# A new table of order for a fused attention and maxout-FFN kernel

## The chip, the core and the metric

The kernel runs on one core of one Trainium2 chip. The metric is the device time of one execution in microseconds (us); a kernel's time is the median of its runs. Lower is better.

## What is computed

Linear attention with learned features, then a feed-forward layer whose hidden value is the maximum of three products.

```
# q, k, v: (8, 8, 576, 64); w_phi: (64, 128)
proj = x @ w_phi                               # x is q or k
proj = proj - max(abs(proj), axis=-1)
phi  = concat(exp(proj), exp(-proj))           # 256 features
kv   = phi(k).T @ v;  z = sum(phi(k))
attn = phi(q) @ kv / (phi(q) @ z + 1e-6)       # per head
x    = attn as (4608, 512)
h    = maximum(maximum(x @ w1, x @ w2), x @ w3)   # 512 -> 768
out  = h @ w_out                               # 768 -> 512, float32
```

## The kernel before

**Units and stages.** Attention works in 16 units of four heads (half of a batch's eight), 18 tiles of 128 rows each. Of a unit, q, k and v are loaded; q and k are made bf16 and transposed into `qkT` (units 0 to 3 on PE at L494 and L497, with q and k of units 1 to 3 loaded straight into bf16 by POOL's queue at L463; later units by a cast on POOL at L480 and a transposing DMA at L512). PE projects (`G`, L535, into `psq` and `psk`), DVE takes the maxima (L554), ACT the exponentials of k (`Ek`, L548), POOL multiplies v by the rows' scale `em` (L589, into `vab`), PE forms `kvps` (`K`, L643: 72 matmuls of 65 columns), PE projects q once more (`M`, L614 to L619, into `psm`) with the maximum taken off, ACT takes the exponentials `Eq` (L627), PE multiplies by kv (`N`, L661, 10 matmuls into `psn`), DVE divides (L667, L668, into `x_sb`). The result is turned into `xT`, for units 0 and 1 on PE (`X`, L681) and a copy (L684), later by a transposing DMA (L691).

**The feed-forward part** runs over nine chunks of 512 tokens: one per batch (tokens 0 to 511 of 576) and one of all the rests. It uses max(a, b, c) = a + max(0, b - a, c - a). So w2 and w3 become differences with w1 (`wd`, L784, three instructions each, in place in `w_bf`), and w1 times w_out is formed once (`wt`, L798 and L801; `wm`, L812). A chunk has a first pass of six tiles with w2 - w1 (`up`, L714, evacuated with a relu at L722 or L724), a second with w3 - w1 (`up2`, L714, evacuated at L720), and per 128 tokens 4 matmuls with w1·w_out (L741) and 6 with w_out (L746) into one bank, a copy (L754) and a store (L761). Chunk 0 needs units 0 and 1 in `xT`, and the differences.

**What sets the order.** The program first makes a list of nodes (a node is a group of instructions on one engine, with its data and buffers). Then `plan` (L251) reads the table `PLAN`: each word is a node's number, a letter for its engine (T is PE, D DVE, A ACT, G POOL, S SP's queue), a digit for each buffer or PSUM bank that it is the first to use, and behind the @ a planned start. The words' sequence is the order in which the instructions are written, and so the order of each engine, which works in order; nothing is reordered on the chip. The planned starts are used for one thing more: where they leave PE a gap, `fill` writes matmuls on constant data (`idler`, L843), which keep PE running.

```
for word in PLAN.split():
    what, start = word.split("@")
    at = next(i for i, c in enumerate(what) if c.isalpha())
    n, slots = nodes[int(what[:at])], iter(what[at + 1:])
    n.eng, n.start = {"T": "PE", "D": "DVE", "A": "ACT", "G": "POOL", "S": "SP"}[what[at]], float(start)
    ...
    order.append(n)
```

**Loads.** SP's queue brings the raw q, k and v (L449, L474); POOL's queue brings q and k of units 1 to 3 (L463) and the four weight matrices (L421) with a cast to bf16. v of units 1 to 3 waits for a one-element copy on DVE (L472) that reads `qkT` of the unit before.

Of the kernel before, what the change touches and what calls it, by code (L numbers as in the profile page):

```python
# [105 lines left out]
1078G@20.80 106A@20.83 108D@20.83 70T070@20.95 96A@21.32 160D2@21.44 167D@21.54 161S@21.69 94D@21.76 109D@21.98 100T64@22.05
296S0@22.17 115T53@22.27 101A@22.52 72D@22.59 362S1@22.65 1094T2@22.75 119D@22.96 102A@23.02 117A@23.50 104D@23.66 116A@23.84
1096T0@24.05 107A@24.18 103D@24.26 124A1@24.68 118D@24.87 120A@24.93 127G1@25.07 71A@25.18 1095D@25.21 183T003400@25.44
1097A@25.59 173T16@25.66 168T57@25.88 123A@26.09 177D@26.13 1098T2@26.23 185A@26.24 170A@26.73 186D@26.74 125G@27.00 175A@27.22
176D@27.35 137T01@27.52 184A@27.71 171D@27.95 77T30@27.98 126G@28.12 138A@28.23 1092T1@28.29 78D0@28.56 139A@28.71 172D@29.18  # L110
1099A@29.20 122G@29.23 79T5@29.58 174A@29.70 187D@29.79 75T3@29.90 1093A@30.18 140T0@30.21 121G@30.35 229D3@30.39 131T2@30.44
76D1@30.50 141A@30.69 73T6@30.89 142A@31.03 80D0@31.11 128T4@31.21 132A@31.37 11G@31.47 364G0@31.62 74D1@31.73 178T13@31.76
133A@31.85 143T105@31.98 130A@32.34 181D@32.35 129A@32.82 182D@32.96 188T26@33.08 233T1@33.31 145A@33.33 192D@33.57 144A@33.73
134T4@33.88 191D@33.91 196A0@34.13 234D0@34.25 146T51@34.34 190A@34.38 198G0@34.53 148T0@34.65 135A@34.72 147D0@34.90
235T2@35.06 231T1@35.17 189A@35.20 149D1@35.52 199A@35.55 136A@35.70 152T5@35.74 193T6@36.05 232D@36.14 179A@36.18 81T0@36.29
83T4@36.60 197G@36.62 169A@36.67 153D0@36.76 150T1@36.91 194A0@37.16 154T7@37.31 236D@37.38 180A@37.41 195S@37.56 151D1@37.60
242T115611@37.72 84A@37.90 247T23@38.05 155D@38.22 297S0@38.34 156T1@38.39 82D@38.69 230S@38.82 215T047@38.87 157A@38.95
1080D@39.16 426S1@39.30 249A@39.60 1081D@39.78 1104T0@40.09 244A@40.09 1082D@40.40 248A@40.58 1106T1@40.95 250D@41.02 216A@41.07
365G@41.37 251D@41.63 1102T4@41.81 1107A1@42.06 246D@42.23 1105A@42.56 366S1@42.64 1110T2@42.67 245D@42.84 243A@43.06
1084D@43.45 1108T3@43.54 1103A@43.55 1111A@44.05 1085D@44.07 252T10@44.50 217A@44.55 1083D@44.69 257T56@44.72 237T42@44.83  # L120
1109A@44.95 1112T7@45.17 240D@45.31 259A@45.45 299G2@45.66 239A@45.79 255D@45.91 1124T3@46.04 254A@46.28 1113D@46.52 253A@46.77
1422G@46.78 1116T4@46.90 260D@47.13 300G@47.18 238A@47.26 1125D@47.47 556S0@47.65 258A@47.75 209T10@47.76 262T7@47.98
1118T5@48.04 241D@48.09 263A1@48.29 429G1@48.30 211A@48.54 264S@48.69 261D@48.70 212T3@48.90 203T7@49.01 210A@49.02 1117D@49.04
1120T2@49.23 363S0@49.47 204A@49.51 1119D@49.66 427S1@49.95 205A@49.99 200T6@50.09 256D@50.28 1122T1@50.30 214A@50.48
1121D@50.89 265A1@51.04 206T4@51.17 213A@51.29 266G1@51.44 367T005700@51.48 1123D@51.51 202A@51.63 301S2@51.63 382T02@51.70
1114T3@52.04 201A@52.11 386D@52.17 370D@52.78 1130T1@52.91 384A@52.93 1115D@53.39 208A@53.42 267G@53.53 224T60@53.77 207A@53.91
371D@54.01 220T5@54.08 383A@54.39 275T31@54.40 1131T@54.61 385D@54.62 369A@54.88 225D0@55.22 368A@55.37 1101G@55.62 221D1@55.84
276A@55.86 222T4@55.90 491S1@56.07 218T2@56.22 1132A0@56.35 223D0@56.47 272T0@56.53 278T6@56.74 268G@56.82 273A@56.99
372T75@57.06 219D1@57.09 430G@57.10 284T114@57.28 277A@57.48 376D@57.70 226S@57.85 274A@57.96 375D@58.31 377T23@58.38 280A@58.45
1126T0@58.72 286D@58.92 279A@58.93 380D@59.30 373A@59.42 281T7@59.58 387T46@59.79 285D@59.91 282A@59.94 269T2@60.06 1127T@60.27  # L130
283A@60.28 381D@60.29 431S0@60.52 271A@60.62 391D@60.89 270A@61.11 390D@61.23 293T11@61.56 395A0@61.59 374A@61.84 291T7@61.87
396G0@61.99 294D0@62.12 289T4@62.19 379A@62.33 1134T2@62.50 290D1@62.75 1128A1@62.82 287T5@63.36 292D0@63.37 388A@63.43
1138T1@63.68 378A@63.77 288D1@63.99 397G@64.08 389A@64.26 317T114011@64.64 295S@64.76 302T73@64.86 312T65@65.08 319A@65.11
320D@65.11 1135T@65.42 313A@65.60 321D@65.75 303A@66.09 559G0@66.18 316D@66.35 304A@66.58 1139T@66.71 557S0@66.88 305D@66.96
1136A2@67.07 398G@67.30 298S1@67.36 306D@67.57 1100G@67.58 314A@67.68 392T4@68.00 307T72@68.16 318A@68.17 315D@68.17
414T053@68.38 308A@68.66 1140D3@68.78 309A@69.15 393D0@69.40 322T06@69.48 310D@69.60 1142T1@69.71 394S@69.75 323A@69.84
324A@70.18 311D@70.21 416A@70.52 622S1@70.53 1154T4@70.57 560G@70.68 325D@70.82 1143A0@70.92 1129S@71.01 326D@71.16 415A@71.42
# [12 lines left out]
461G@91.60 353D1@91.66 572T47@91.79 1170T2@92.13 574A@92.26 359D0@92.28 579A@92.75 357D1@92.90 1171T@93.00 573A@93.24 575D@93.52  # L150
# [724 lines left out]
```

## Time and profile before

| | |
|---|---|
| median of 3 runs | 285.09 us (285.10, 285.09, 283.02) |
| span of the profiled execution | 282.5 us, first to last instruction; no other time of that execution is on the page |
| busy: PE, weight loads, DVE, ACT, POOL | 96%, 54%, 75%, 68%, 40% |
| granted TensorE clock | 1.000 |
| HBM | 34.64 MB read, 9.44 MB written, 156 GB/s over the span |

A row of a group or of the timeline names the line, the engine, the operation and out<-in; behind it stand the idle time of the engine ahead of it and what ended that. PEld is PE's loading of weights, which overlaps its matmuls. "issue" is time in which the engine waited for nothing that the profile shows. SPq, POOLq and ACTq are the issuing of DMAs.

### The profile page before, as it was taken

What the parts mean: (1) busy time and instruction counts of PE and PEld (TensorE: products, weight loads), DVE (VectorE), ACT (ScalarE), POOL (GpSimd) and SP (SyncE); (2) the same over time, 40 slices, a digit from 0 to 9 for tenths busy, and PEclk for the clock granted to TensorE, in tenths of its full rate; (3) what the DMA queues carried; (4) which work ended last, traced back from release to release, by engine and by line L of the source; (5) the groups of instructions that cost most, each with busy time, mean ns of one, the idle gap of its engine ahead of it and who ended that gap; (6) DMA issues with size and microseconds to landing.
All of it is one profiled execution on the core that took longest, in us unless ns stands there. A gap on an engine that the chain in (4) does not pass through costs nothing.

```text
span 282.5 us, 8556 instructions
## 1 busy us (share of the span) xinstructions
PE 271.2 (96%) x3521; PEld 154.0 (54%) x3560; DVE 211.6 (75%) x443; ACT 192.3 (68%) x449; POOL 113.2 (40%) x106
## 2 busy tenths in 40 slices
PE   8888979999999999999999999999999999999995
PEld 3565764566555644764556456555455465444443
DVE  4998989998877888679989876997477594254141
ACT  2897979898889779998585879977707961311111
POOL 8373567748176418913760563053033600000000
PEclk9999999999999999999999999999999999999999
DMA  7999999888999999999797866954975105600154
GB/s 202 240 206 282 280 273 240 266 204 167 300 363 198 175 308 300 194 165 277 212 199 129 246 235 124 166 102 167 186 177 116 40 4 104 137 2 0 37 123 139
DMA packets 68337, 51.45 MB, mean 182 GB/s; under 512 B 48778, under 2 KB 53066, under 8 KB 68298
## 3 DMA queue, kind: packets, MB, share of 16 engines
q1 hardware_dynamic: 63876, 45.74, 66.8%
q0 software_dynamic: 4000, 4.92, 10.0%
q8 instruction: 28, 0.46, 0.7%
q10 hardware_dynamic: 422, 0.24, 0.3%
q14 instruction: 11, 0.09, 0.1%
HBM read 34.64 MB, written 9.44 MB: 156 GB/s over the span
## 4 chain that ended last, share of the span: by engine, by line
PE 80%; DMA 11%; DVE 4%; issue 2%; SPq 1%; DVEq 0%
PE ups L714 31%; PE ops L746 14%; PE ops L741 10%; DMA wout_bf<-in_moe_w_out_dram 6%; PE psn L661 6%; PE kvps L643 5%; PE psm L614 5%; PE psq L535 4%; PE pm L812 2%; DMA out_dram<-osb 2%; DMA xT<-x_sb 2%; DVE x_sb L668 2%; DMA k_raw<-in_k_dram 1%; DVE mqp L554 1%; DVE mk L554 1%
## 5 line engine op out<-in xcount | busy, mean ns | idle before, releaser
L714 PE MATMUL ups<-xT,w_bf 128*128 128x512 bf16 x416 | 100.3, 379 | 1.4 <-DMA xT<-x_sb 0.3
L589 POOL TENSOR_TENSOR vab<-v_raw,em 128x1152 bf16<-128x1152 f32 (+1 forms) x36 | 68.2, 1907 | 67.2 <-ACT em L585 50.9
L548 ACT ACTIVATE Ek<-psk 128x512 bf16<-128x512 f32 (+1 forms) x160 | 80.8, 569 | 13.9 <-PE psk L535 10.1
L627 ACT ACTIVATE Eq<-psm 128x512 bf16<-128x512 f32 (+1 forms) x160 | 79.2, 570 | 7.3 <-PE psm L614 7.0
L714 PEld LDWEIGHTS <-w_bf 128*128 128x128 bf16 x432 | 41.0, 98 | 47.4 <-issue 0.4
L554 DVE TENSOR_REDUCE mqp<-psq 128x4 bf16<-128x512 f32 (+1 forms) x80 | 48.8, 631 | 6.3 <-PE psk L535 4.4
L746 PE MATMUL ops<-wout_bf,hT 128*128 128x512 bf16 (+2 forms) x215 | 49.3, 367 | 1.0 <-issue 0.5
L554 DVE TENSOR_REDUCE mk<-psk 128x4 f32<-128x512 f32 (+1 forms) x80 | 48.5, 628 | 2.4 <-PE psk L535 1.7
L720 DVE TENSOR_TENSOR hT<-hT,ups 128x512 bf16<-128x512 bf16 x54 | 36.1, 682 | 16.4 <-PE ups L714 12.7
L668 DVE TENSOR_TENSOR x_sb<-psn,rden 128x320 bf16<-128x320 f32 x64 | 31.5, 492 | 2.2
L746 PEld LDWEIGHTS <-hT 128*128 128x128 bf16 x228 | 21.1, 98 | 21.7
L722 ACT ACTIVATE hT<-ups 128x512 bf16<-128x512 f32 x33 | 19.1, 603 | 17.3 <-PE ups L714 15.8
L661 PEld LDWEIGHTS <-Eq 128*128 128x128 bf16 x640 | 25.0, 97 | 7.8 <-ACT Eq L627 0.2
L754 DVE COPY osb<-ops 128x512 f32<-128x512 f32 (+1 forms) x22 | 14.7, 669 | 16.8 <-PE ops L746 16.0
L661 PE MATMUL psn<-kv_sb,Eq 128*128 128x65 bf16 x640 | 26.9, 194 | 0.2 <-DVE mqp L554 0.2
L754 ACT COPY osb<-ops 128x512 f32<-128x512 f32 (+2 forms) x16 | 8.9, 562 | 23.2 <-PE ops L746 22.6
L741 PE MATMUL ops<-xT 128*128 128x512 bf16 x90 | 24.1, 380 | 0.3
L535 PE MATMUL psq<-w,qkT 64*128 64x128 bf16 x288 | 24.3, 217 | 0.1
L535 PE MATMUL psk<-w,qkT 64*128 64x128 bf16 x288 | 24.0, 217 | 0.4 <-ACT Eq L627 0.4
L535 PEld LDWEIGHTS <-qkT 64*128 64x128 bf16 x576 | 16.5, 94 | 12.0 <-issue 8.9
L614 PE MATMUL psm<-qkT,wphi_m 128*128 128x512 bf16 (+1 forms) x70 | 22.1, 358 | 0.0
L480 POOL CAST qk_bf<-q_raw 128x1152 bf16<-128x1152 f32 x12 | 13.8, 1147 | 20.3 <-DMA out_dram<-osb 9.4
(73 smaller groups left out, 230.9 us busy)
## 6 DMA issues: line engine op xcount, KB each, us to landing
v_raw<-in_v_dram SPq DMA_DIRECT2D x16, 576.0 KB
out_dram<-osb SPq DMA_DIRECT2D x64, 128.0 KB
q_raw<-in_q_dram SPq DMA_DIRECT2D x12, 576.0 KB
k_raw<-in_k_dram SPq DMA_DIRECT2D x12, 576.0 KB
w_bf<-in_moe_w_dram POOLq DMA_DIRECT2D x3, 768.0 KB, 20.3
qk_bf<-in_k_dram POOLq DMA_DIRECT2D x3, 288.0 KB, 13.9
qk_bf<-in_q_dram POOLq DMA_DIRECT2D x3, 288.0 KB, 13.4
wout_bf<-in_moe_w_out_dram POOLq DMA_DIRECT2D x1, 768.0 KB, 17.7
```

The lines of the kernel that those rows point to most:

```text
L535: nc.tensor.matmul(ps()[:, i, :], lhsT=cols[r, :], rhs=w2[r, c, :], start=True, stop=True)
L548: nc.scalar.activation(Ek[s]()[:, tiles_of(t0, n), :], of(1), EXP, scale=1.0 - 2.0 * s)
L554: nc.vector.tensor_reduce((mq, mk)[c]()[:, tiles_of(t0, n)], of(c), AXX, ALU.max, apply_absolute_value=True)
L589: (nc.vector if n_.eng == "DVE" else nc.gpsimd).tensor_tensor(vab()[:, g, t0:t1, 0:D], vb()[:, t0:t1, :], em()[:, g, t0:t1].unsqueeze(2).t ...
L614: nc.tensor.matmul(psm()[:, 0:w], lhsT=wphi_m, rhs=rhs, start=True, stop=True)
L627: nc.scalar.activation(Eqb()[s][:, cols], psm()[:, 0:w], EXP, scale=1.0 - 2.0 * s)
L661: nc.tensor.matmul(psn()[:, c, :], lhsT=Eqb()[g][:, t0:t0 + P], rhs=kv()[:, pr, ab, g, :], start=(g == 0), stop=(g == 1))
L668: nc.vector.tensor_tensor(x_sb()[:, pr, :, ab, :], psn()[:, :, 0:D], rden().to_broadcast([P, 5, D]), ALU.mult)
L714: nc.tensor.matmul(ups(), lhsT=w_bf[i + 1][:, ct, j * P:(j + 1) * P], rhs=tokens_of(ct), start=(ct == 0), stop=(ct == CT - 1))
L720: nc.vector.tensor_tensor(hT()[:, j, :], hT()[:, j, :], ups(), ALU.max)
L741: nc.tensor.matmul(ops_()[:, 0:width], lhsT=tile_of(ct, tt), rhs=line_w[c_i > MOVE][:, ct, cols], start=(ct == 0), stop=False)
L746: nc.tensor.matmul(ops_()[:, 0:width], lhsT=hT()[:, j, tt * P:(tt + 1) * P], rhs=wout_bf[:, j, cols], start=False, stop=(j == JT - 1))
```

## The change

Only the table is replaced. The new one was found by a search of small moves in plays of the program in which each transfer comes as late against plan as it did in a trace. Stages, tiles, buffers and every line of code are as before. A line of each, with the word for the load of w2 (node 1077):

```
-49G@14.45 41D@14.56 65A@14.63 43A@15.12 99D@15.16 110T67@15.27 63A@15.46 50G@15.57 55T5@15.61 98D@15.77 1077G@15.85 111A@15.94
...
+1093A@29.53 186D@29.89 77T6@29.97 138A@30.03 1077G@30.27 128T0@30.29 174A@30.52 78D1@30.54 178T47@30.86 129A@31.02 365G0@31.07
```

Of 1478 nodes 110 change engine: of the relus of the first pass 30 stand on DVE (21 before) and 24 on ACT (33), of the copies of L754 16 on DVE (22) and 22 on ACT (16), of the 14 copies to `mT` 10 on DVE (2), and the three `wd` of w3 on POOL (all six on DVE before).

On POOL, where w2 and w3 are loaded (the last two rows of L421), before:

```order
L589 TENSOR_TENSOR vab<-v_raw,em 128x9x64
L599 CAST vab<-em 128x2x9
L421 DMA w_bf<-in_moe_w_dram 128x4x768
L589 TENSOR_TENSOR vab<-v_raw,em 128x9x64 x2
L599 CAST vab<-em 128x2x9
L421 DMA w_bf<-in_moe_w_dram 128x4x768
L599 CAST vab<-em 128x2x9
L589 TENSOR_TENSOR vab<-v_raw,em 128x9x64 x4
```

The same place now, up to the differences of w3:

```order
L463 DMA qk_bf<-in_q_dram 128x2x576
L599 CAST vab<-em 128x2x9
L589 TENSOR_TENSOR vab<-v_raw,em 128x9x64 x4
L421 DMA w_bf<-in_moe_w_dram 128x4x768
L480 CAST qk_bf<-k_raw 128x18x64
L421 DMA w_bf<-in_moe_w_dram 128x4x768
L480 CAST qk_bf<-q_raw 128x18x64
L589 TENSOR_TENSOR vab<-v_raw,em 128x18x64 x2
L599 CAST vab<-em 128x36
L787 CAST gated<-w_bf 1x1 x3
L784 TENSOR_TENSOR w_bf<-w_bf 128x4x256 x3
```

Both loads moved behind unit 1's four multiplications, the second behind a cast too, and three subtractions came to POOL; one load of unit 3 (first row) also moved back, from ahead of unit 0's multiplications.

On DVE, from the last copies to `xT` to the reductions of unit 3, before:

```order
L684 COPY xT<-pxT 128x576 x2
L784 TENSOR_TENSOR w_bf<-w_bf 128x4x256 x3
L554 TENSOR_REDUCE mqp_80<-psq 128x4
L554 TENSOR_REDUCE mk<-psk 128x4 x2
L554 TENSOR_REDUCE mqp_80<-psq 128x4
L784 TENSOR_TENSOR w_bf<-w_bf 128x4x256 x3
```

And now:

```order
L554 TENSOR_REDUCE mqp_80<-psq 128x4
L784 TENSOR_TENSOR w_bf<-w_bf 128x4x256 x2
L554 TENSOR_REDUCE mk<-psk 128x4
L472 CAST v_raw<-qkT 1x1
L784 TENSOR_TENSOR w_bf<-w_bf 128x4x256
L554 TENSOR_REDUCE mk<-psk 128x4
```

The copies to `xT` went to ACT, the differences of w2 stand between reductions of unit 3, and those of w3 are gone from here.

On PE, rows 1213 to 1220 of its order (loads and matmuls counted from 0), in the turning of units 0 and 1; `Eq_1_77` and `Eq_1_78` are unit 1's exponentials of q. Before:

```order
L681 LDWEIGHTS x_sb
L681 MATMUL pxT<-ident,x_sb 128x128
L681 LDWEIGHTS x_sb
L681 MATMUL pxT<-ident,x_sb 128x128
L681 LDWEIGHTS x_sb
L681 MATMUL pxT<-ident,x_sb 128x128
L661 LDWEIGHTS Eq_1_77
L661 MATMUL psn<-kv_sb,Eq_1_77 128x65
```

Rows 1209 to 1216 now:

```order
L681 LDWEIGHTS x_sb
L681 MATMUL pxT<-ident,x_sb 128x128
L843 LDWEIGHTS idle
L843 MATMUL idler<-idle 128x512
L843 LDWEIGHTS idle
L843 MATMUL idler<-idle 128x512
L661 LDWEIGHTS Eq_1_77
L661 MATMUL psn<-kv_sb,Eq_1_77 128x65
```

Unit 0's ten transposes ran in one go before the last `N` of unit 1; now one group of five stands before another `N`, and two idlers between the second group and the last `N`.

More of the change, by code (lines that the diff above doesn't have):

```diff
@@ L106 @@
[L106 to L113, printed above, removed]
@@ new lines @@
+1160T1@79.91 328D1@80.01 403A@80.16 1159D@80.21 329S@80.36 407A@80.65 1156T0@80.78 1161D@81.03 686S1@81.06 404A@81.13
+622S1@81.52 406A@81.62 411T4@81.65 1162T7@81.77 1157D@81.90 494G@82.04 409A@82.10 333A@82.59 399T6@82.64 1163D@82.89
+349T115@82.96 401A@83.11 561S1@83.11 400A@83.62 452T20@84.00 412A@84.10 437T37@84.12 455D@84.37 350A@84.44 1174T6@84.45
+456D@84.71 413A@84.84 441D@85.05 351A@85.18 334T21@85.32 1175T@85.54 440D@85.66 439A@85.81 336A@86.30 335A@86.80 428S3@86.83
+346T1@86.84 419T40@86.96 1176D0@87.09 337T5@87.28 438A@87.29 343T3@87.50 420D0@87.71 1166T2@87.72 348A@87.78 1177S@87.86
@@ new lines @@
+1023A@205.52 1020D@205.76 1339T@205.83 1021D@206.36 1019A@207.12 1330T6@207.13 1340D1@207.38 1028A@207.61 1030D@208.00
+1327T@208.00 1341S@208.15 1025D@208.61 1031D@209.22 872T4@209.30 876T0@209.62 873D0@209.87 1331T@209.94 1029A@209.97
+877D1@210.49 1328D0@211.11 880S@211.26 1037T24@211.34 999T050@211.46 1038A@211.71 1040D@211.73 1018A@212.05 1032T12@212.50
+1332A3@212.54 1329S@212.76 1334T7@212.83 1035D@212.98 1024A@213.15 1041D@213.59 1335T@213.70 1036D@213.93 1039A@214.08
+1001A@214.42 1034A@214.82 1348T1@215.00 1336D2@215.25 990T61@215.87 1026D@215.87 1337S@216.02 1346T4@216.09 1045A1@216.62
@@ new lines @@
+1000A@216.87 996T0@216.96 1046G1@217.02 1350T7@217.08 1347D1@217.21 1333S@217.22 1349A@217.27 998A@217.77 984T3@217.95
+1042T5@218.17 1351D@218.20 1342T4@218.23 986A@218.42 1043D1@218.81 1344T1@219.10 1047G@219.12 1044A@219.16 1343D@219.35
+997A@219.86 1061T70@219.97 1052T5@220.09 1033A@220.20 1345D@220.22 1352T4@220.31 1053A@220.69 992A@221.17 993T1@221.18
+1428G@221.21 1354T0@221.40 1048G@221.61 1054A@221.66 991A@222.14 1064T125@222.36 1353A@222.63 995A@223.13 1362T6@223.49
+1065D@223.65 1066A@223.65 1355D@224.03 985A@224.05 1058T4@224.36 1062A@224.54 1055T2@224.58 1364T5@224.80 1057A@225.05
@@ new lines @@
+1389D@258.48 1434T3@259.10 1401D@259.11 1411T@259.97 1435D@260.22 1438T6@261.27 1412A0@261.52 1415T@262.14 1413S@262.28
+1439A@262.39 1444T1@263.44 1381S@263.48 1416A2@263.69 1440T4@264.31 1417S@264.68 1446T6@265.18 1441D@265.43 1419T@266.05
+1447D@266.30 1445D@266.92 1450T3@267.35 1420A3@267.60 1454T5@268.22 1421S@268.36 1451D@268.47 1453D@269.09 1458T4@269.09
+1459T@269.96 1455T@271.26 1460A0@271.51 1461A@272.14 1407T@272.56 1456D1@272.81 1457S@273.58 1462T6@273.86 1408D2@274.11
+1463T@274.73 1409S@274.88 1470T1@276.03 1471T@276.25 1464A3@276.28 1466T2@276.58 1472D0@276.83 1465A@276.91 1467T@277.01
@@ L245 @@
+1473A@277.51 1474T3@277.66 1475T@277.88 1468D1@277.91 1469S@278.45 1476A2@278.45 1477A@278.72
 """
```

265 lines of the change are left out of this document (126 added, 139 removed).

## The prediction

> **What bounds the kernel now.** I read the page first, then the busy time by stretch, then single rows.
>
> ```profile
> span 282.5 us, 8556 instructions
> PE 271.2 (96%) x3521; PEld 154.0 (54%) x3560; DVE 211.6 (75%) x443; ACT 192.3 (68%) x449; POOL 113.2 (40%) x106
> PE   8888979999999999999999999999999999999995
> PEclk9999999999999999999999999999999999999999
> 0.00:41.78 41.78, 36.75 (x715) 24.75 (x718) 34.53 (x84) 31.74 (x77) 24.00 (x33) 1.00 1.07 245
> 41.78:240.00 198.22, 195.40 (x2615) 110.42 (x2643) 162.21 (x337) 153.64 (x361) 88.84 (x74) 1.00 0.82 192
> 240.00:279.00 39.00, 38.79 (x196) 18.67 (x199) 14.56 (x22) 6.80 (x13) 0.33 (x1) 1.00 0.29 70
> 250.00:260.00 10.00, 9.95 (x47) 4.56 (x47) 4.40 (x7) 2.28 (x4) 0.00 (x0) 1.00 0.00 0
> ```
>
> The last four rows are stretches: start and end, length, then busy us and instructions of PE, PEld, DVE, ACT, POOL, then clock, DMA share and GB/s. The clock granted is 1.00, so pace is a matter of waiting alone. A busy PE is not yet a PE at its peak, since records of matmuls overlap; so I price the work by the distance from one matmul to the next and count weight loads.
>
> ```profile
> L714 PEld LDWEIGHTS <-w_bf 128*128 128x128 bf16 x432 | 41.0, 98 | 47.4 <-issue 0.4 <-DVE mk L554 0.2 <-DVE mqp L554 0.2
> L746 PEld LDWEIGHTS <-hT 128*128 128x128 bf16 x228 | 21.1, 98 | 21.7
> L661 PEld LDWEIGHTS <-Eq 128*128 128x128 bf16 x640 | 25.0, 97 | 7.8 <-ACT Eq L627 0.2 <-issue 0.2
> L643 PEld LDWEIGHTS <-Ek 64*128 64x128 bf16 x1152 | 18.8, 94 | 2.0 <-issue 1.0 <-ACT Ek L548 0.8
> L535 PEld LDWEIGHTS <-qkT 64*128 64x128 bf16 x576 | 16.5, 94 | 12.0 <-issue 8.9 <-DVE qkT L500 1.3 <-DVE mk L554 0.4
> 222.46 2.59 PE ups L714 x12
> 30.41 0.62 PE psn L661 x20
> 84.14 1.10 PE kvps L643 x72
> 26.39 0.05 PE psq L535
> 278.81 0.50 PE L746 MATMUL ops<-wout_bf,hT 128*128 128x128 bf16 x6
> ```
>
> A matmul of 512 columns costs 2.59/12 = 0.216 us, one of L661 0.031, 72 of L643 1.10, a pair of L535 about 0.055. There are 870 wide ones (432 of L714, 210 of L746, 140 of L741, 88 of L614, L616 and L812): 187.8 us. L661 gives 19.8, L643 17.6, L535 15.8, and the narrow rest, at these prices by its columns, 13.4. **PE's work is 254.4 us.** PE ends at 279.3 (278.81 + 0.50), so 24.9 us are empty (idlers of L843 count as empty). Counted the same way, 24.9 us of work stand ahead of the first row of L714, which comes at 41.78: 16.9 us are empty there, and 8.0 in the 237.5 us behind. From 250 to 260 there is none (47 loads in 10 us is one in 0.213). So this kernel is a PE that starts late and then runs full. An order can gain from three places: the 16.9, the 8.0 and the tail of 3.2 behind PE's end.
>
> The Trainium skill, "Perfetto Trace Analysis", section "Identifying the Most-Contended Engine", takes the share of weight loads for the measure of PE's headroom, not matmul busy time. By that, 54% leaves nearly half of the span to win and PE would not be the bound. The stretch 250:260 speaks against it: PEld shows 4.56 of 10 us there while the wide matmuls follow each other without a hole. I give that reading no chance.
>
> **The change, part by part.** The same instructions run, save for choices of engine. PE's 254.4 us stay: 0.
>
> *The start.* What holds the first L714 is a chain through one stop:
>
> ```profile
> 36.87 0.45 PEld L681 LDWEIGHTS <-x_sb 128*128 128x128 bf16 x8
> 38.74 0.33 PE L681 MATMUL pxT<-ident,x_sb 128*128 128x128 bf16 x3 [1.30 <-issue]
> 38.91 0.47 PE L661 MATMUL psn<-kv_sb,Eq 128*128 128x65 bf16 x10
> 39.65 0.49 DVE L668 TENSOR_TENSOR x_sb<-psn,rden 128x320 bf16<-128x320 f32 x1
> 40.20 0.45 PE L681 MATMUL pxT<-ident,x_sb 128*128 128x128 bf16 x5
> 40.69 0.64 ACT L684 COPY xT<-pxT 128x576 bf16<-128x576 bf16 x1 [0.94 <-PE pxT L681]
> 40.78 1.88 DVE L784 TENSOR_TENSOR w_bf<-w_bf 128x1024 bf16<-128x1024 bf16 x3
> 42.01 0.81 PE L714 MATMUL ups<-xT,w_bf 128*128 128x512 bf16 x3 [0.16 <-issue]
> q8 instruction: 28, 0.46, 0.7%
> ```
>
> PE stands 1.30 us between the eighth and ninth load of L681, for nothing that the profile shows; the last division, the last copy to xT and the first L714 all follow from it. PE's order has 7122 rows, which is 27.8 times 256, and queue q8 moved 28 packets of instructions: I read the stop as PE waiting for its next packet, at the ninth load's row, 1215. In the new order row 1215 is the first load of the last `N` of unit 1, right behind two idlers. Idlers are written only where the table leaves PE a gap, so the stop there lies at least partly beside a wait that is due anyway. Bounds: 0 (the stop returns in full) and -1.3 (hidden in full); the new place is between the two, I take **-0.7**. If that cover is missing, the term is 0.
>
> The Trainium skill, "Runtime: NRT & Kernel Launch", section "Instruction fetch mechanics", agrees with blocks of 256 instructions but calls the crossing mostly hidden. By it the stop would be something else and its place no reason for a gain, and the sum would lack the -0.7.
>
> ```profile
> L648 ACT CAST kv_sb<-kvps 128x260 bf16<-128x260 f32 x17 | 6.3, 383 | 0.5 <-PE kvps L643 0.4
> L648 DVE CAST kv_sb<-kvps 128x260 bf16<-128x260 f32 x15 | 6.2, 418 | 0.5 <-PE kvps L643 0.5
> ```
>
> Ahead of that last division DVE has 61 of the table's entries before and 60 after; ahead of the last copy to xT ACT has 69 and 69. What changes sides between them is a kv copy (0.42 on DVE, 0.38 on ACT) and a handful of copies of that kind. Both ends: half a us either way; I take 0.
>
> *Weights.* w2 and w3 are issued on POOL, now far later:
>
> ```profile
> 1.89 0.94 POOL L463 DMA_DIRECT2D qk_bf<-in_k_dram  x1
> 15.53 0.82 POOL L421 DMA_DIRECT2D w_bf<-in_moe_w_dram x1
> 20.76 0.81 POOL L421 DMA_DIRECT2D w_bf<-in_moe_w_dram x1
> 26.51 4.48 POOL L589 TENSOR_TENSOR vab<-v_raw,em 128x576 bf16<-128x576 f32 x4 [1.48 <-DMA v_raw<-in_v_dram]
> 31.06 1.14 POOL L480 CAST qk_bf<-q_raw 128x1152 bf16<-128x1152 f32 x1
> DMA to landing us min/median/max: 12.2/20.3/20.7
> q0 software_dynamic: 4000, 4.92, 10.0%
> ```
>
> They landed some 20.3 to 20.7 us after issue, near 36 and 41.3. Now they stand behind the four L589 of unit 1: issue at 31.0 (26.51 + 4.48) and, behind a cast of 1.14 and an issue of 0.82, 33.0. How long they then take is not shown. Upper end: 20.5 again, landing at 51.5 and 53.5. Lower end: the queue, which moved its 4.92 MB from its first issue at 1.89 to 41.3 (0.125 MB/us, so 6.3 us for one matrix of 0.79 MB), is empty by then. The first matrix landed 12.2 us after its issue with 0.59 MB of q and k ahead; (0.59 + 0.79)/0.125 = 11.0, which leaves 1.2 to start. So w2: 31.0 + 1.2 + 6.3 = 38.5; w3: 44.8. I take the lower end, for the old 20 us were mostly other transfers ahead in that queue, and those have gone. w2 is first read at 40.78: 2.3 us to spare, 0. What waits in line behind its reader on DVE, should it be late, are the reductions of unit 3.
>
> *The differences of w3* go from DVE (three at 0.68, row below) to POOL.
>
> ```profile
> L784 DVE TENSOR_TENSOR w_bf<-w_bf 128x1024 bf16<-128x1024 bf16 x6 | 3.8, 680 | 0.0
> L589 POOL TENSOR_TENSOR vab<-v_raw,em 128x1152 bf16<-128x1152 f32 x28 | 59.1, 2124 | 62.6 <-ACT em L585 47.8 <-DMA v_raw<-in_v_dram 12.3 <-issue 2.5
> 40.00:50.00 10.00, 9.79 (x139) 5.39 (x136) 9.89 (x19) 8.28 (x19) 6.33 (x11) 1.00 0.98 250
> ```
>
> POOL's price for this isn't in the trace; from 0.68 (DVE's) to 2.12 (POOL on 1152 columns), nearest 2.12 x 1024/1152 = 1.9. From 44.8 they end at 46.7, 48.6 and 50.5. Six tiles of 0.86 and three groups of L535 (0.5 together) behind 41.8 bring PE to the second pass over L714 at 47.5; it needs the first at once, the second one tile later (48.4), the third some three tiles after that: nearly on time, **+0.3** for a transfer that lands a little late (ends 0 and +3). Behind them on POOL wait the casts of unit 4, whose transposed DMA is wanted far later. DVE, full at 9.89 of 10 us there, loses 2.0 us of work; PE lost little in that stretch, so 0.
>
> *Behind 42.* 8.0 us empty in 237.5, in pieces of 0.1 to 0.4: a new order scatters them anew. Ends -2 and +2, value 0. *Tail:* the last copies and stores change between ACT and DVE, SP and ACT; the old tail after PE's end was 3.2 us. **-0.1**, ends -0.3 and +0.3.
>
> Sum: -0.7 + 0.3 - 0.1 = -0.5, span **282.0 us**. The page gives no time of its own for the profiled execution beside the span; the three runs are 285.10, 285.09 and 283.02, the median 2.6 above the span. 282.0 + 2.6 = **284.6 us**.
>
> **Rivals.**
> 1. *Slower: w2 or w3 lands late.* The search held each transfer to the lateness traced in its old place; these two now travel beside other loads. The place is DVE's first L784 (w2) and POOL's three (w3); up to 40.8 and 44.6 it costs nothing, from there each us late is a us of PE, which has no other work in its order. For it: software-queue loads took 20 us, and the DMA share was 1.07 up to 41.78. Against it: fewer transfers ahead. Late by 4 us, in place of the 0.3, they give 288.3; with the full 20.5 us (w2 at 51.5, 10.7 late) 295.0.
> 2. *Faster: the start is freed.* The stop is hidden in full (-1.3), DVE's 2.0 us less let the first stages through one us earlier, and 1 us of the 8.0 goes: -3.3, 281.8. For it: DVE at 9.89 of 10. Against: ACT's and PE's work ahead of the first L714 are unchanged.
> 3. *It doesn't do what it says, no gain:* the stop returns wherever row 1215 stands and w3 costs its 0.3: 285.3. Same class as my forecast.
> 4. *PE starves behind 42* because an order made for one set of landings meets another: +2 and more small holes, 287 to 288.
>
> **How the numbers follow.** The forecast and rival 3 have 0.74 together (own range 282.8 to 286.8), rival 1 0.13, rival 2 0.08, rival 4 0.05. One per cent, about what a measurement of this kernel tells from no change, is 2.85 us: faster means below 282.2 (rival 2, and a sliver of mine), slower above 287.9 (rival 1 and a part of 4). That makes 0.09, 0.76 and 0.15. The range reaches to rival 2 and to the nearer price of rival 1: 281.8 to 288.4.
>
> **What would show it.** First L714 at 40.5 to 42; no PE stop of over 1 us on L681, one beside L661's first load of that `N` if at all; w2's and w3's landing 8 to 12 us after issue; PE ends near 278.8; PE busy 96% again. I am wrong if DVE waits for a DMA at L784, if POOL's L784 ends after 49 with PE standing at L714, or if stretches behind 42 show PE under 9.6 of 10.

## The result, and the profile after

| | before | after |
|---|---|---|
| median of 4 runs | 284.27 us (283.02 to 285.10) | 296.29 us (294.02 to 298.22) |
| span of the profiled execution | 282.5 us | 295.0 us |
| ratio after / before | | 1.041, 95% interval 1.034 to 1.047 |

The new table is 4% slower. The forecast was 284.6 us, no change, with a range up to 288.4: wrong by 12 us. Of the ratios below, that of e17 leaves out its two runs far above the fastest, while a median leaves out none.

The page of after: span, shares, PE's forty slices, and the chain that ended last by engine. Then two groups, two stretches as they were cut for before (up to the first L714, and the middle), and PE's last row.

```profile
span 295.0 us, 8590 instructions
PE 275.2 (93%) x3562; PEld 153.5 (52%) x3562; DVE 211.8 (72%) x447; ACT 193.7 (66%) x443; POOL 117.6 (40%) x105
PE   8889889998999989999989799999998899999995
PE 67%; DMA 18%; DVE 10%; POOL 1%; issue 1%; ACT 1%; POOLq 0%; SPq 0%
L714 PE MATMUL ups<-xT,w_bf 128*128 128x512 bf16 x432 | 102.7, 379 | 5.4 <-DMA xT<-x_sb 5.4
L681 PE MATMUL pxT<-ident,x_sb 128*128 128x128 bf16 x20 | 1.8, 220 | 0.0
0.00:43.91 43.91, 37.65 (x720) 24.79 (x721) 35.78 (x86) 34.08 (x77) 26.11 (x37) 1.00 1.05 223
43.91:250.00 206.09, 196.16 (x2638) 109.00 (x2633) 159.49 (x336) 153.52 (x355) 91.09 (x67) 1.00 0.77 185
291.39 0.50 PE L746 MATMUL ops<-wout_bf,hT 128*128 128x128 bf16 x6
```

PE's share fell from 96% to 93%, at the same granted clock. In the middle PE lacks 9.93 of 206.09 us; before it lacked 2.82 of 198.22. PE ends at 291.9, so with its 254.4 us of work 37.5 are empty, 12.6 more than before; counted as in the prediction (24.9 us of work ahead, and 0.1 for unit 2's first L614, which now stands there too), 18.9 of them lie ahead of the first L714 (16.9 before) and 18.6 behind it (8.0 before). **Most of the loss is behind 42.** What PE waits for, in total, times and the longest; two pieces of the chain (start and length) that are the flight of such a transfer, of unit 2's maxima and unit 4's x; and four of the waits in the timeline with the issue that each waits for:

```profile
PE ups L714 <- DMA xT<-x_sb: 5.4, 5, 2.1
PE psm L614 <- DMA qkT<-mT: 1.9, 2, 1.0
...
37.58 4.86 DMA qkT<-mT
...
101.73 4.16 DMA xT<-x_sb
...
144.41 0.74 ACTq L570 DMA_DIRECT2D qkT<-mT  x1
148.81 0.38 PE L614 MATMUL psm<-qkT,wphi_m 128*128 128x512 bf16 x1 [1.39 <-DVE mqp L554]
164.02 2.04 SPq L691 DMA_TRANSPOSE xT<-x_sb  x1
169.16 1.46 PE L714 MATMUL ups<-xT,w_bf 128*128 128x512 bf16 x6 [2.06 <-DMA xT<-x_sb]
221.99 2.36 SPq L691 DMA_TRANSPOSE xT<-x_sb  x1
227.22 1.04 PE L714 MATMUL ups<-xT,w_bf 128*128 128x512 bf16 x4 [1.24 <-DMA xT<-x_sb]
231.19 0.77 ACTq L570 DMA_DIRECT2D qkT<-mT  x1
233.15 0.50 PE L614 MATMUL psm<-qkT,wphi_m 128*128 128x256 bf16 x2 [0.85 <-DMA qkT<-mT]
```

PE stands for 0.9 to 2.1 us at a time in front of its first matmul behind a small transfer: that of x to `xT`, and that of q's maxima (`mT`) into a row of `qkT`. In before the only such wait among PE's is this:

```profile
PE ups L714 <- DMA xT<-x_sb: 0.3, 1, 0.3
```

The wait at 148.81 is put down to a reduction on DVE, but it is of this kind: unit 9's maxima were issued at 144.41, and the wait is gone below once PE reads neither. In the order of the rows the six took 4.9, 4.2, 4.4, 5.1, 5.2 and 2.0 us. The table shows that PE was given less time. The words of unit 15's transfer (node 1044) and of its first reader on PE (1061), old and new:

```
-1044S@220.41   1061T20@226.44
+1044A@219.16   1061T70@219.97
```

The planned room between them, 6.0 us in the old table, is 0.8 in the new one. For the six (maxima of unit 2, x of 4, maxima of 9, x of 9 and 12, maxima of 15) the old table left 10.2, 5.3, 4.6, 4.1, 5.6 and 6.0 us, the new one leaves 3.8, 3.9, 2.8, 3.3, 3.7 and 0.8. A short room alone does not tell where PE will stand: the maxima of units 3, 7, 11 and 12 have 3.0, 3.3, 3.5 and 3.4 us in the new table and x of unit 15 has 2.4, and PE waited for none of these maxima and 0.5 us for that x.

### The profile page after: what moved, and what is told of

It reads as the page before. It is cut to its first block, busy times and chain, and to the rows that moved or that the text cites. A ratio compares the mean times of both kernels' runs of the same rounds, so it can differ in the third digit from the quotient of the medians.

```text
span 295.0 us, 8590 instructions
## 1 busy us (share of the span) xinstructions
PE 275.2 (93%) x3562; PEld 153.5 (52%) x3562; DVE 211.8 (72%) x447; ACT 193.7 (66%) x443; POOL 117.6 (40%) x105
## 4 chain that ended last, share of the span: by engine, by line
PE 67%; DMA 18%; DVE 10%; POOL 1%; issue 1%; ACT 1%; POOLq 0%; SPq 0%
PE ups L714 28%; PE ops L746 11%; PE ops L741 9%; DMA qk_bf<-in_q_dram 8%; DMA xT<-x_sb 8%; PE psn L661 5%; PE kvps L643 5%; PE psm L614 4%; PE psq L535 4%; DVE mqp L554 2%; DMA qkT<-mT 2%; DVE mk L554 2%; DVE x_sb L668 2%; DVE hT L720 2%; PE tps L497 1%
## 5 line engine op out<-in xcount | busy, mean ns | idle before, releaser
L714 PE MATMUL ups<-xT,w_bf 128*128 128x512 bf16 x432 | 102.7, 379 | 5.4 <-DMA xT<-x_sb 5.4
L548 ACT ACTIVATE Ek<-psk 128x512 bf16<-128x512 f32 (+1 forms) x160 | 83.4, 570 | 20.4 <-PE psk L535 11.2
L714 PEld LDWEIGHTS <-w_bf 128*128 128x128 bf16 x432 | 40.5, 98 | 52.4 <-issue 3.6
L746 PE MATMUL ops<-wout_bf,hT 128*128 128x512 bf16 (+2 forms) x228 | 52.2, 368 | 0.0
L754 ACT COPY osb<-ops 128x512 f32<-128x512 f32 (+1 forms) x22 | 12.9, 585 | 34.2 <-PE ops L746 28.7
L724 DVE TENSOR_SCALAR hT<-ups 128x512 bf16<-128x512 f32 x30 | 20.6, 687 | 19.3 <-PE ups L714 19.2
L661 PE MATMUL psn<-kv_sb,Eq 128*128 128x65 bf16 x640 | 28.1, 194 | 0.0
L722 ACT ACTIVATE hT<-ups 128x512 bf16<-128x512 f32 x24 | 14.1, 606 | 18.2 <-PE ups L714 17.2
L614 PE MATMUL psm<-qkT,wphi_m 128*128 128x512 bf16 (+1 forms) x70 | 22.9, 358 | 3.2 <-DMA qkT<-mT 1.9
L741 PE MATMUL ops<-xT 128*128 128x512 bf16 x96 | 24.5, 379 | 0.0
L643 PE MATMUL kvps<-vab,Ek 64*128 64x65 bf16 x1152 | 20.4, 190 | 2.0 <-DVE mk L554 1.4
## 6 DMA issues: line engine op xcount, KB each, us to landing
w_bf<-in_moe_w_dram POOLq DMA_DIRECT2D x3, 768.0 KB, 11.7
```

The costliest lines, as they stand in the source:

```text
L548: nc.scalar.activation(Ek[s]()[:, tiles_of(t0, n), :], of(1), EXP, scale=1.0 - 2.0 * s)
L643: nc.tensor.matmul(kvps[ab]()[:, t // NT, g, :], lhsT=Ek[g]()[r, t, :], rhs=vab()[r, g, t, :], start=(t + g == 0), stop=(t == UT - 1 and g ...
L661: nc.tensor.matmul(psn()[:, c, :], lhsT=Eqb()[g][:, t0:t0 + P], rhs=kv()[:, pr, ab, g, :], start=(g == 0), stop=(g == 1))
L714: nc.tensor.matmul(ups(), lhsT=w_bf[i + 1][:, ct, j * P:(j + 1) * P], rhs=tokens_of(ct), start=(ct == 0), stop=(ct == CT - 1))
L741: nc.tensor.matmul(ops_()[:, 0:width], lhsT=tile_of(ct, tt), rhs=line_w[c_i > MOVE][:, ct, cols], start=(ct == 0), stop=False)
L746: nc.tensor.matmul(ops_()[:, 0:width], lhsT=hT()[:, j, tt * P:(tt + 1) * P], rhs=wout_bf[:, j, cols], start=False, stop=(j == JT - 1))
```

## The experiments

Ratios are to the old kernel, run on the same chip between the others. A table whose words were recombined had its buffers and PSUM banks given out anew where they clashed.

### Which part of the change: halves, engines, loads

**e1** is the old table's first 232 words (to 38.4 us of its plan), then the rest in the new order; **e2** the new table's first 232, then the old order; **e3** the new sequence with all 110 nodes back on their old engines; **e4** the old table up to 174 us (1070 words), then the new order. Of the diffs, three words of e3 (e1, e2 and e4 are the two tables joined at a seam):

```diff
-1087A@17.82
+1087D@17.82
-12D@4.38
+12A@4.38
-1095A@25.48
+1095D@25.48
```

> The old table's first 232 words (planned starts up to 38.7 us), then all remaining nodes in the new table's order and on its engines. Theory R (the order behind 40 us gives PE steps that are fed by a transfer or by DVE too little room): 292 to 295, with the first L714 near 41.8 and some 18 us of PE empty behind it. Theory S (the later loads of w2, w3 and of unit 3's q, and the start that is 2.2 us later, set everything behind it late): 284 to 286. Theory E (relus, copies and subtractions on other engines): 292 to 295.

Measured: 306.91 us, ratio 1.077 (1.068 to 1.086).

> The mirror image: the new table's first 232 words (up to 39.3 us), then the remaining nodes in the old table's order and on its engines. Theory R: 285.5 to 288 (only the start's 2.2 us). Theory S: 293 to 297. Theory E: 285.5 to 288.

Measured: 300.25 us, 1.054 (1.047 to 1.062). Both are slower than either whole table, so they say nothing on which half is at fault: each half meets banks and landings that it was not made for (in e2 PE waits 1.1 us at L741 for a bank that DVE's copy still holds).

> The new table's sequence, but each of the 110 nodes that changed engine goes back to its old engine. Theory E: 285 to 288. Theories R and S: 293 to 298.

Measured: 295.82 us, 1.039 (1.029 to 1.048), as the new kernel. The engines are not the cause.

> The old table's first 1070 words (up to 174 us), then the rest in the new order. Theory R: 287 to 289 (the new order shows 5.6 us of PE empty behind 174 us, the old one 1.4). Theory S: 284 to 285. Theory E: 286 to 288.

Measured: 292.03 us, 1.025 (1.017 to 1.034). PE in two stretches, first of before, then of e4, then of the new kernel (start and end, length, busy us of PE; the rest as above):

```profile
41.78:174.00 132.22, 129.93 (x1787) 73.76 (x1805) 113.44 (x234) 110.37 (x262) 72.61 (x61) 1.00 0.96 231
174.00:279.50 105.50, 104.56 (x1031) 55.46 (x1041) 63.44 (x127) 50.23 (x113) 16.55 (x13) 1.00 0.46 98
...
43.00:174.00 131.00, 128.68 (x1780) 73.27 (x1801) 111.96 (x232) 109.76 (x259) 70.86 (x58) 1.00 0.95 229
174.00:289.00 115.00, 106.33 (x1023) 55.02 (x1033) 65.09 (x130) 48.65 (x108) 16.57 (x13) 1.00 0.45 92
...
43.91:174.00 130.09, 123.13 (x1686) 68.60 (x1682) 103.81 (x215) 103.91 (x242) 67.67 (x48) 1.00 0.92 231
174.00:292.00 118.00, 114.45 (x1174) 60.11 (x1166) 72.18 (x147) 55.48 (x125) 23.82 (x20) 1.00 0.45 96
```

Up to the seam PE lacks 2.3 us in both; behind it 0.9 in the old order and 8.7 in e4. So a loss arises behind 174 that is not carried over from the start. But the new kernel itself lacks 7.0 us up to 174 and only 3.6 behind: some 5 of the 8.7 are not its own, and are likely the seam's, as in e1 and e2. That e4 took longer than every theory expected fits this.

**e5** is the old table with three POOL loads (q of unit 3, w2, w3) moved to the new table's late places; **e6** the new table with the same three moved back to the early ones. Of e5:

```diff
-227G1@10.01
-1077G@15.85
-1078G@20.80
+227G@25.30
+1077G@31.45
+1078G@32.80
```

And of e6:

```diff
-227G@24.68
-1077G@30.27
-1078G@32.19
+227G1@10.02
+1077G@15.85
+1078G@20.80
```

> The old table with three words of POOL moved back to where the new table has them: a load of unit 3, w2 and w3 (issues near 25, 31 and 33 us instead of 10.7, 15.5 and 20.8). Nothing else changes. Theory S (these late loads cost the time): 292 to 297. Theory R (room behind 40 us): 284.5 to 287, the start alone, with a wait of 1 to 2 us for unit 3's load and w3's differences on DVE late by at most 2.

Measured: 284.83 us, 1.000 (0.997 to 1.004).

> The new table with the same three words moved forward to the old places on POOL. Theory S: 284 to 287. Theory R: 293 to 295, better by the 1.3 us that PE waits for unit 3's q and no more.

Measured: 300.06 us, 1.053 (1.043 to 1.064). Late loads cost the old order nothing, early ones don't help the new: they are not the cause either. Most of what e6 took beyond the new kernel (3.8 us) is clock: in its trace the granted clock fell to 0.5 twice, for 3.4 us each, behind stops of 2.0 and 1.3 us at L643; the waits for x and for maxima are still there (5.1 and 2.9 us).

### More room at every transfer

**e7** raises in the new table the planned room ahead of PE's readers to at least 5.0 us for maxima and x and 8.0 us for the transposing DMA of q and k (54 of PE's places change); **e8** does so with e6's loads.

```diff
-1061T70@219.97
+1061T70@224.16
```

> The new table with PE's steps behind a transfer put back: a step that reads qkT's row of maxima stands at least 5.0 us of planned time behind the issue of its transfer (the new table goes down to 0.8, the old to 3.9), a chunk's first pass at least 5.0 behind its xT transfer (2.4, old 4.0), a projection at least 8.0 behind its transposing transfer (5.4, old 7.6); what hangs on them follows, 54 places of PE's order change. Theory R: 286 to 290, PE's waits for DMA at L714 and L614 (9 us) nearly gone. Theory S: 294 to 297.

Measured: 302.50 us, 1.066 (1.054 to 1.079).

> Both edits of the new table, early loads and room. Theory R: 285 to 289. Theory S: 284 to 287 whatever the room does. If both are wrong (the loss is spread over steps that wait for DVE and ACT): 290 to 294.

Measured: 307.80 us, 1.081 (1.072 to 1.089). Both got slower, though PE's waits for x and the maxima fell (e7 below; its table is a line longer, so its lines count one more):

```profile
PE ups L715 <- DMA xT<-x_sb: 0.8, 1, 0.8
...
PE psm L615 <- DMA qkT<-mT: 0.4, 1, 0.4
L844 PE MATMUL idler<-idle x51: 376/379/635, 1.0 to 257.4; 128*128 128x512 bf16 x51
```

The last row shows a fault of the edit: later planned starts leave gaps in PE's plan, and the program fills such gaps with idlers, 51 in place of 26, which is 25 x 0.216 = 5.4 us more for PE. e18 repeats it without.

### PE freed from the transfers

Four kernels let PE read other data, in place, so that it need not wait; all transfers still run, nothing is moved. **e9** (new order) and **e10** (old) leave out the reading of x and of the maxima, **e11** and **e12** also that of `qkT` by the projections.

```diff
-        chunk(b, units[2 * b]["done"] + units[2 * b + 1]["done"], lambda ct, b=b: xT[:, b, ct, 0:SM],
-              lambda ct, tt, b=b: xT[:, b, ct, tt * P:(tt + 1) * P],
+        chunk(b, units[2 * b]["done"] + units[2 * b + 1]["done"], lambda ct: xT[:, 0, ct, 0:SM],
+              lambda ct, tt: xT[:, 0, ct, tt * P:(tt + 1) * P],
...
-                    nc.tensor.matmul(psm()[:, 0:w], lhsT=wphi_m, rhs=rhs, start=True, stop=True)
+                    nc.tensor.matmul(psm()[:, 0:w], lhsT=wphi_m[0:D, :], rhs=rhs[0:D], start=True, stop=True)
```

In e11 and e12 also:

```diff
-    cols = qkT()[:, t * P:(t + 1) * P]
+    cols = qkT()[:, t * P:(t + 1) * P] if by_pe else xT[:, 0, 0, 0:P]
```

> New order, nothing moved. Left out: from chunk 1 on, the first matrices read chunk 0's tokens in xT, so PE waits for no transfer of x to xT; and the feature matmul of units 2 to 15 (L614) contracts the 64 rows of qkT without the row of maxima, so PE waits for no transfer of mT to qkT. All transfers still run. Theory R (the loss is PE standing before steps whose transfer lands after the planned time): the six jumps of lateness at such steps go, 1.1 (V of unit 2) + 1.65 (x of chunk 2) + 1.5 (V 9) + 2.0 (chunk 4) + 1.4 (chunk 6) + 1.0 (V 15) = 8.65 us, so 286.5 to 289 and a DMA wait of under 0.5 us at L714. Theory D (the loss is made upstream, by vector and scalar work that runs late, and the transfer is only where it is seen): PE waits at the next step instead, 293 or more. Theory U (PE's work itself got slower, no single waits): 296.

Measured: 294.09 us, 1.037 (1.033 to 1.040).

> Old order with the same two things left out, as the control. Theory R: nothing waits for such a transfer in the old order behind 42 us (no step there adds over 0.3 us), so no gain beyond 1 us: 283.5 to 285. If freeing the transfers gives the old order several us as well, what e9 gains is no sign of the new order's loss.

Measured: 293.16 us, 1.032 (1.030 to 1.035).

> As the run of the new order with x and V freed, and in units 4 to 15 the projections (L535) also take their columns from chunk 0's xT in place of qkT, so PE waits for no transposing DMA of q and k, nor for the POOL casts and raw loads behind it. Theory R: the jumps at the first projection of unit 4 (1.3) and unit 12 (1.1) go as well: 284 to 287. Left over are the late start (2.2 us up to the first L714) and the wait of K of unit 6 for raw v (0.7). Theory D: no further gain, 291 or more.

Measured: 295.40 us, 1.040 (1.034 to 1.047).

> Old order with the same three things left out, as the control: 283 to 285 by theory R, whose old order has no waits to win back.

Measured: 292.89 us, 1.031 (1.027 to 1.035). The controls did not hold: the old order lost 9 us from waiting for less. PE is 97% busy, but its matmuls take longer. In e10:

```profile
PE 282.9 (97%) x3560; PEld 151.2 (52%) x3560; DVE 212.7 (73%) x443; ACT 193.6 (66%) x449; POOL 113.1 (39%) x106
...
206.28 0.82 PE L614 MATMUL psm<-qkT,wphi_m 64*128 64x512 bf16 x3
207.03 1.04 PE L714 MATMUL ups<-xT,w_bf 128*128 128x512 bf16 x4
207.99 0.28 PE L614 MATMUL psm<-qkT,wphi_m 64*128 64x256 bf16 x1
```

Three matmuls of 512 columns take 0.75 us (0.65 at 0.216 each), four 0.96 (0.86): each change between 64 and 128 rows costs 0.10 us. The edit made L614 a matmul of 64 rows, and PE's old order has 84 more such changes (164 in e10's trace, 80 in that of before); 9.1 us of loss / 84 = 0.108. The Trainium skill, "TensorEngine Tiling (Array Packing)", section "Key Properties", says that changing the tiling mode drains TensorE; it gives no price, these rows do. With such changes in both (102 more in the new order), e9 and e10 differ by only 0.9 us (294.09 and 293.16) in place of 12, e11 and e12 by 2.5. That speaks for the transfers, but a PE slowed by 9 us also hides other lateness. So the same without the change of rows: **e13** (new order) and **e14** (old) keep 128 rows and let L614 read a landed part of `xT`; **e15** is the new order with x alone freed.

```diff
-    nc.tensor.matmul(psm()[:, 0:w], lhsT=wphi_m, rhs=rhs, start=True, stop=True)
+    nc.tensor.matmul(psm()[:, 0:w], lhsT=wphi_m, rhs=xT[:, 0, 0, 0:w], start=True, stop=True)
```

> New order, nothing moved. Left out: from chunk 1 on, L714 and L741 read chunk 0's tokens in xT, and the feature matmul of units 2 to 15 (L614) reads columns of chunk 0's xT, 128 rows as before, in place of qkT; PE so waits for no transfer of x and none of maxima, all of which still run. Theory R (the loss is PE standing before these transfers): the 8.65 us of jumps at such steps go, 286 to 289. Theory D (late vector and scalar work upstream, only seen there): 293 or more, with the waits at the next evacuation, kv or Eq. Both with the start 2 us late as in the new order.

Measured: 286.10 us, 1.005 (1.002 to 1.009).

> Old order with the same left out, as the control without the cost of 64 rows: 283 to 285 in both theories (no wait of over 0.3 us at such a step there). If it is 290 or more again, the matmuls themselves changed and e13 must be read against it.

Measured: 284.66 us, 0.999 (0.996 to 1.002).

> New order with the tokens alone left out as above (qkT is read as it should be). Theory R: the 5.05 us of jumps at the first matrix of chunks 2, 4 and 6 go, 290 to 292.5, less what the V steps behind them then wait (1 to 2 us): 290 to 294. Theory D: 294 or more.

Measured: 291.37 us, 1.023 (1.016 to 1.030). The page of e13, and its waits of PE:

```profile
span 283.3 us, 8585 instructions
PE 274.7 (97%) x3562; PEld 154.1 (54%) x3562; DVE 211.3 (75%) x447; ACT 192.7 (68%) x443; POOL 117.6 (42%) x105
PE 77%; POOL 7%; DMA 5%; issue 5%; DVE 5%; ACT 0%; POOLq 0%
...
PE kvps L643 <- POOL vab L599: 1.1, 1, 1.1
```

This decides it. Freed from these two kinds of transfer, and with them from the work that feeds them, the new order comes back from 296.3 to 286.1 (three of its ten runs took 288.9 to 291.5), and the old one does not move. Hardly any wait took their place (the longest is 1.1 us, once, for `vab`): DMA went from 18% to 5% of the chain, DVE from 10% to 5%. Freeing x alone gives 4.9 of the 10.2 us, and the waits for maxima grow to 4.5 us in the trace:

```profile
PE psm L614 <- DMA qkT<-mT: 4.5, 3, 2.4
```

A part of what e15 lacks is clock: its runs took 292.68 and 292.53 us at a granted clock of 0.994 and 0.988, and 290.21 and 289.80 at 1.000 and 0.999.

### The converse: transfers that land later in the old order

**e16** is the old table with each transfer of x issued twice.

```diff
             def xdma():
-                nc.sync.dma_start_transpose(
+                for _ in range(2):
+                    nc.sync.dma_start_transpose(
```

> Old order, nothing left out, but each transfer of x to xT is issued twice in a row by SP (the second writes the same values), so that PE's first matrix of each chunk gets its tokens about 1.4 us later (the issue's own 1.3 to 2.1 us on SP in the old trace). Rooms from issue to PE in the old trace: 5.0, 5.3, 4.0, 4.0, 4.8, 5.4 and 4.8 us for the last transfer of chunks 1 to 7. Theory R: each of these steps waits some 1 to 1.5 us, 6 to 10 us in all with what SP issues behind: 289 to 294, with a DMA wait at L714 of 5 us or more. Theory D: the transfers have slack or it is made up for: under 287.

Measured: 321.31 us, 1.129 (1.123 to 1.135). Far more than expected, for two reasons that the trace shows. The issue of unit 6's x in before and the pair of issues in e16, PE's waits in e16, and PE in three stretches of 2 us around one of them (start and end, length, busy us of PE, PEld, DVE, ACT, POOL, granted clock, DMA share, GB/s):

```profile
118.21 1.97 SPq L691 DMA_TRANSPOSE xT<-x_sb  x1
...
129.44 6.53 SPq L692 DMA_TRANSPOSE xT<-x_sb  x2
...
PE ups L715 <- DMA xT<-x_sb: 23.3, 7, 4.7
...
108.00:110.00 2.00, 0.00 (x0) 0.00 (x0) 0.00 (x0) 0.92 (x2) 0.00 (x0) 1.00 0.91 165
110.00:112.00 2.00, 1.32 (x4) 0.50 (x5) 0.00 (x0) 0.00 (x0) 0.00 (x0) 0.60 0.89 247
112.00:114.00 2.00, 2.00 (x7) 0.74 (x6) 0.89 (x2) 0.00 (x0) 0.00 (x0) 0.55 0.93 229
```

One issue takes 1.3 to 2.4 us in both runs, but SP starts the second of a pair 3.4 to 6.0 us behind the first, so x lands that much later, not 1.4. Such a transfer landed 3.4 to 4.8 us after its issue, and SP waits on semaphores 24 times at this line (13 before): it looks as if the program holds the second write of a tile back until the first has landed. Each of the seven chunks then waits 3.3 us on average (23.3/7), against 0.3 us in all before: most of the lateness of this transfer goes to PE. And behind five of the seven stops (those of 2.7 to 4.7 us) the granted clock falls, here to 0.55 to 0.60 in two rows of 2 us, a loss of 2 x (0.40 + 0.45) = 1.7 us; all such rows of the trace, added up in this way, make 10.2. 23.3 and 10.2 are 33.5 of the span's 36.5 us more (319.0). The Trainium skill, "TensorE: Matmul & The Clock Gate", section "Part 1: The HAM clock gate", says that PE's clock is halved after an idle window of about 3.4 us, until PE has been busy for as long; the fall agrees in depth and length, but shorter stops can be enough. In the new kernel, where no wait was over 2.1 us, the clock stayed at 1.00, while e15 has a stop of 2.38 us (in the stretch from 39.9 to 42.2) with half the clock behind it:

```profile
42.24 0.28 PE L614 MATMUL psm<-qkT,wphi_m 128*128 128x256 bf16 x1 [2.38 <-DMA qkT<-mT]
...
44.00:46.00 2.00, 2.00 (x15) 0.80 (x10) 0.69 (x1) 1.15 (x3) 1.87 (x1) 0.50 0.95 213
```

The length alone does not decide it: a stop of 2.05 us in e17 was followed by such a fall, one of 2.13 us in e16 was not.

### Repairs

**e17** gives only the six steps named above more room in the new table, **e18** repeats e7; neither adds idlers. Two of e17's words, and the line that keeps idlers out of both:

```diff
-668T10@140.79
-1061T70@219.97
+668T10@142.54
+1061T70@222.66
-        if n.eng != "PE":
+        if n.eng != "PE" or n.start > 39.6:
```

> New order, nothing left out; only six steps get more room between the start of the transfer and PE's first step that reads it, PE doing other work of its order first: maxima of unit 2 from 3.8 to 5.0 us, of unit 9 from 2.75 to 4.5, of unit 15 from 0.8 to 3.5; x of unit 4 from 3.9 to 5.2, of unit 9 from 3.25 to 5.0, of unit 12 from 3.7 to 5.0 (16 of PE's 651 places and 7 of ACT's change; no idlers added). Theory R with a local cause: most of the 8.65 us of waits at these steps go, 287 to 291. Rival (joint schedule: what is pulled ahead instead or read later makes others wait): 293 or more.

Measured: 297.31 us, 1.032 (1.022 to 1.042).

> The run with more room at all such steps, again, without the 25 idlers that were written into PE's order for it. If the idlers were its loss beyond the new order's: 302.5 - 5.4 = 297 or less, and by theory R, whose waits at the transfers were down to 1.2 us there, 288 to 294. If the moved steps were its loss (joint schedule): 299 to 303.

Measured: 300.29 us, 1.060 (1.052 to 1.069). e17 can't be told from the new kernel, and its runs spread from 291.75 to 300.88. The spread goes with the granted clock: 1.000 at 291.75, then 0.994 at 295.54, 0.988 at 299.08 and 0.983 at 300.88. The trace is of the last. In it the waits for maxima fell (0.8 us for `mT`), those for x did not, and the clock fell behind its two longest stops, at x of units 4 (2.7 us) and 9 (2.05 us):

```profile
PE ups L715 <- DMA xT<-x_sb: 6.5, 5, 2.7
...
100.00:110.00 10.00, 6.41 (x111) 3.18 (x111) 4.50 (x9) 4.04 (x10) 7.06 (x6) 0.73 0.93 238
```

At full clock the six rooms may thus win back some 4 us of the 12; one run without a trace does not show it. In e18 the idlers are gone and most of e7's loss is still there. Its waits:

```profile
PE ups L715 <- DMA xT<-x_sb: 3.8, 4, 1.5
PE kvps L644 <- ACT Eq L628: 1.3, 2, 1.0
PE psn L662 <- ACT Eq L628: 1.3, 2, 1.1
```

PE waits for ACT where the new kernel did not, and still for x. Moving readers alone does not mend such a table; that each engine's order is tied to the others' is how I read it, and these runs do not show it further.

## Why the prediction was wrong

**The step that failed is the one headed "Behind 42": "a new order scatters them anew. Ends -2 and +2, value 0".** It measured +10.6: 18.6 us empty behind the first L714 against 8.0. The mechanism was among the rivals, as the fourth ("PE starves behind 42 because an order made for one set of landings meets another"), at +2 and a chance of 0.05. The size was wrong because I took it from the pieces of the old trace, 0.1 to 0.4 us each. Those are what is left when every reader comes after its transfer. The size of a hole where a reader comes first is set by something else, the room in the plan against the time that the transfer takes; the room could be read beforehand, from two words of the table. The time could only be bounded, since in before each reader comes after its transfer: at most 4.0 us from issue to reader for x of units 7 and 9, 3.9 for the maxima of unit 13. Against these bounds all six new rooms are short, by 0.1 us at units 2 and 4 and by more at 9, 12 and 15. So are five more, where PE then waited 0.5 us at most: the table would have told the danger, not the places. In all, the six rooms fell short of what the transfers then took by 7.5 us (1.1, 0.3, 1.6, 1.8, 1.5 and 1.2; the first, unit 2's, lies ahead of the first L714). e13 against e14 shows that waiting for x and the maxima carries 10.6 of the 12.0 us (12.02 less the 1.44 that is left). That the rooms in the table, and not late work ahead of the transfers, set these waits is argued from the words and not shown by a run.

The other terms, in their order:

- *PE's work, 254.4 us, unchanged, and PE the bound:* right. e13 with the same work in the new order has a span of 283.3.
- *The start, -0.7 for the stop in L681:* the stop is gone in after (0.0 us ahead of L681's matmuls) and there in the old order's other traces (1.5 us in e5), as forecast; that it was a wait for instructions, no run shows. The gain did not come: the first L714 stands at 43.91, outside the 40.5 to 42 given, with 2.0 us more empty ahead of it. A load of unit 3 (1.11) and the maxima of unit 2 (1.00) were waited for in its place:

```profile
35.62 0.64 PE L497 MATMUL tps<-ident,qk_bf 128*64 128x128 bf16 x16 [1.11 <-DMA qk_bf<-in_q_dram]
42.49 0.28 PE L614 MATMUL psm<-qkT,wphi_m 128*128 128x256 bf16 x1 [1.00 <-DMA qkT<-mT]
43.91 4.49 PE L714 MATMUL ups<-xT,w_bf 128*128 128x512 bf16 x20
```

  How much of the 2.0 belongs to the new order stays open: in e13, where PE does not wait for the maxima, the first L714 stands at 41.39, and in e5 the old order's first L714 stood at 43.61 at an unchanged median.
- *The weights, +0.3:* right. w2 and w3 were issued at 31.61 and 33.52 (31.0 and 33.0 forecast), the loads of this group landed 11.7 us after issue by the median (8 to 12), POOL's differences began at 45.25 (44.8) and took 2.1 us each, the upper bound in place of the 1.9 taken. They ended at 51.5, past the 49 named as a warning, but PE did not wait for them:

```profile
w_bf<-in_moe_w_dram POOLq DMA_DIRECT2D x3, 768.0 KB, 11.7
31.61 0.82 POOL L421 DMA_DIRECT2D w_bf<-in_moe_w_dram  x1
33.52 0.74 POOL L421 DMA_DIRECT2D w_bf<-in_moe_w_dram  x1
45.25 6.28 POOL L784 TENSOR_TENSOR w_bf<-w_bf 128x1024 bf16<-128x1024 bf16 x3 [0.67 <-DMA w_bf<-in_moe_w_dram]
```

  e5 puts the price of the late loads in the old order at 1.000.
- *The tail, -0.1:* right; 295.0 - 291.9 = 3.1 us in place of 3.2.
- *From span to time, +2.6:* too much; in the profiled run of the new kernel it was 1.8 (296.82 against 295.0).
- *What would show it wrong:* "stretches behind 42 with PE under 9.6 of 10" is the sign that came.

**Open** is what in the new order is late ahead of the transfers and what in their flight: in e13 PE is free of both. At four of the six steps the issue followed within 0.1 us of the data, at x of units 4 and 9 it stood 2.5 and 1.4 us behind other work of SP. Open too is the 1.4 us between e13 and e14, and whether added room can recover the loss. No version ran faster than the old kernel; with these waits taken out altogether the new order only equals it within 0.5%, so these runs show no gain that the waits would have hidden.

## What to carry to other kernels

When a table of order changes under an engine that is full, don't price the rest of the program from the holes that the old trace has. List each transfer that this engine waits for, compare the planned room to its first reader with the time that such transfers took in the trace, and take the sum of the shortfalls as what is at risk: here 7.5 us at six steps came true, while five more short rooms cost next to nothing, and giving the six more room (e17) did not surely bring the time back. Read the granted clock of each run before comparing two of them. And change one thing in a control too: only the old order with the same edit told a removed wait from a matmul that had become slower.

## What the runs showed of the hardware that I had not expected

- A change between matmuls of 64 and of 128 rows costs PE 0.10 us each way; 84 more of them made the old order 9 us slower while PE looked 97% busy (e10).
- Behind a stop of PE of 2.7 to 4.7 us the granted clock fell, in the rows shown to 0.55 to 0.60 over 4 us, which costs another 1.7 us (five times in e16, once for twice as long). Shorter stops were followed by a fall in e15 (2.38 us) and e17 (2.05), and not in the new kernel (2.06) or in e16 (2.13).
